# Attention and a routed expert layer on one core: seven zero stores left out and a new written-out order for the attention phase

## The chip, the cores and the metric

The kernel runs on one NeuronCore of a Trainium2 chip. TensorE (PE; its weight loads are PEld in the profile) multiplies, VectorE (DVE), ScalarE (ACT) and GpSimd (POOL) do the rest, and SyncE (SP) issues most transfers; every engine takes its instructions in the order in which they were written. The metric is device time in microseconds (us) of one execution. Where a profile speaks of the granted clock, 1.00 is TensorE at 2.4 GHz.

## The reference

Attention with four sink keys and a window of 128, then a top-2 mixture of eight experts over its 3072 output rows:

```python
scores = scale * np.matmul(q, k.transpose(0, 1, 3, 2))     # 4 x 8 heads, 768 x 768, D = 64
keep = is_sink | in_window                                 # 4 sinks, window of 128
a = softmax(np.where(keep, scores, -1e9))
x = np.matmul(a, v)  -> (3072, 512)
noisy = x @ w_gate + log1p(exp(x @ w_noise)) * noise       # top 2 of 8 per token
for e in range(8): out[mask] += top2_w * (relu(x[mask] @ w1[e]) @ w2[e])   # 512 -> 1024 -> 512
```

All of it is in float32. On TensorE the experts' products are made of three products of split operands (`w` and its rest, `x` and its rest).

## The kernel before

The kernel has two phases. **Phase one** is attention: 16 pairs of heads (`g`), and for each pair three tiles of 256 query rows, so 48 tiles `n`. A tile goes through `qk` (scores, L404), a copy of the scores to `cbuf` (`prev`, L408 on DVE or L410 on ACT, and `cur`, L426), a maximum (`mins`, L433, DVE), its negative (`minus_max`, L436, POOL), the exponential with its sum (`exps_sums`, L447, ACT), a turn on TensorE (`ptr`, L494), a copy back to `CT` (L408/L410), a masked copy `CM` (L507 on DVE or L510 on POOL), the product with `v` (`pv`, L520 and L523; the latter needs `dv`, the differences of neighbouring blocks of `v`, L310 on POOL), the sinks (L535) and a copy to `xtn` (L408/L410). Rows are then turned (`rows`, L549) and stored to a scratch tensor `x_rows` in DRAM (L554).

Four pairs make one batch of 768 tokens. When a batch is done its logits are made (`proj`, `turn`, L735, L743), and `routing` finds each token's two experts and its rank in each expert's list (DVE, POOL and ACT, some 40 small instructions; `rank` L849/L855 and `place` L944 on TensorE; the one-hot tables `rt_op`, L927, on DVE). Its last transfer, `keep` (L873 to L876), stores the gate weights of the batch in four stores of 128 x 6 runs of 48 bytes each. Rows of the first expert are gathered from `x_rows` by POOL (L1029) while attention still runs. The first weight chunks are loaded too (`st`, L1136) and split (`hi`, L1140, ACT; `lo`, L310, POOL).

**Phase two** is the experts: 16 pieces of up to 512 rows, eight up products (L1184 to L1186) and the down products (L1250 to L1252) in each, with gathers of the next piece's rows and a scatter with addition (L1274) of each result into `out`. `out` has 31 tiles of 128 rows, 24 of tokens and 7 behind the last token, into which the unused slots of a list are scattered; the kernel returns the first 3072 rows alone. Tiles of `out` are set to zero beforehand by stores of a zero tile (`zero`, L1427 to L1429), one per tile of 128 rows: the first `ZEROS` in phase one and the others in phase two.

The order of phase one is written out by hand in three tables. `ORDER` lists the numbers of its operations (transfers included) in the order in which `Plan.replay` emits them; `SIDE` has a 1 where an operation with two possible engines takes the second; `BANKS` gives each PSUM buffer its bank. So each engine's queue, SP's too, is a subsequence of `ORDER`. The durations in the calls of `plan.op` and `plan.dma` move nothing in phase one; the order of phase two is computed from such durations, starting from the times at which `replay` leaves the engines.

Of the kernel before, what the change touches and what calls it, by code (L numbers as in the profile page):

```python
# [27 lines left out]
SLACK = .01  # L28
WARM = 32
FIRST = 4  # L30
ZEROS = 16
EARLY = ((1, 0), (1, 1), (2, 0))
LATE = ((2, 1), (1, 2), (1, 3))

# [1 line left out]
def dram(t, off, ap):  # L36
    return bass.AP(tensor=t.tensor, offset=t.offset + off, ap=ap)


ORDER = """  # L40
# [43 lines left out]
"""  # L84
SIDE = """
11011111100111100110100101101110101110000110111010011001111010010000011000010100011001010000010101111001010001010100
1111000100000100000100000100
"""
BANKS = """
00120120120112001210012001201100211020112001120102021002101012110021102001200110002112102010101211020101210201100210  # L90
0112100112110002012101120201012010120110210110102012
"""


# [667 lines left out]
def routing(nc, plan, cst, sh, b, t0, nt, z, xbuf):  # L762
# [5 lines left out]
    last = T0 + nt == sh.T  # L768
    c, get = cst, plan.get
    gid = b  # L770
# [13 lines left out]
    def t(name):  # L784
        if name in ("oh", "z", "r2"):
            return (name, gid)
        if last and name in ys:
            return ("y", ys[name])
        if name == "lg":
            return ("lg", b)  # L790
        tag = "rt_" + name
        plan.rings.setdefault(tag, 1)
        return (tag, gid)
# [81 lines left out]
            nc.sync.dma_start(dram(xbuf, (T0 + 1) * 128 * sh.XW + q * sh.SW + 128, [[sh.XW, 128], [128 * sh.XW, nt], [1, E + C]]),  # L875
                              rt("w")[:, :, q // 2, :])  # L876

    plan.dma(z if last else plan.now, keep, 1.2, r=[t("w")], w=[("wrow", gid)], n=4)
    most = c["most"]
    ends = last or b in sh.fixed  # L880
    if ends:
        i = b
# [314 lines left out]
def experts(tc, plan, cst, sh, w1, w2, xbuf, out):  # L1197


    nc = tc.nc  # L1200
# [6 lines left out]
    plan.rings.update(gw=2, w1=4, w2a=2, w2b=2, skn=2, sqn=2, wc=2, h=FC + 1, y=4, H=2, Y=4)  # L1207
    scat = {}
    NP = sh.B * sh.H // 2
    zeros = range(ZEROS, out.shape[0] // 128)  # L1210
    UP1, DN1 = DC * 3 * (1 / 2400), .69

    def size(e, t):
# [78 lines left out]
    z = 0  # L1292
# [5 lines left out]
    for q, (e, tiles, width) in enumerate(info):  # L1298
# [34 lines left out]
        for f in range(FC):  # L1333
            k = FC * q + f
            zu = z0 + f * dz if not apart else z0 + f * UP1 * width
            if k >= AHEAD:
                for i in range(DC) if q == 0 else (None,):
                    op("PE", (UP1 * width + .19) / (1 if i is None else DC), zu, lambda q=q, f=f, i=i: up(q, f, i),
                       r=[(x, e, t) for x in ("xh", "xl") for t in tiles] + [w_tile(plan, 1, e, f // 2)[0]], w=[("H", k)],
# [7 lines left out]
        for a, t in enumerate(order):  # L1347
            n = Y[e, t]
            for f in range(FC):
# [3 lines left out]
                   r=[("hh", k), ("hl", k), w_tile(plan, 2, e, f // 2)[0]], w=[("Y", n)], u=[("h", k)])  # L1353
# [72 lines left out]
def zero(plan, nc, cst, sh, out, i, z, r):  # L1426

    plan.dma(z, lambda: nc.sync.dma_start(dram(out, i * 128 * sh.DM, [[sh.DM, 128], [1, sh.DM]]), cst["zt"][:, :sh.DM]),
             .73, r=r, w=[("zero", i)])  # L1429


def phase_one(tc, nc, plan, ac, tail, cst, sh, kq, v, vs, w1, w2, xbuf, out):
# [34 lines left out]
        logits(nc, plan, cst, sh, sh.B - 1, jj, n + PR.get("ll", .5))  # L1467
    first_rows(sh.FA - 1, PR.get("ga_l", 0), PR.get("gt_l", 0))
    for i in range(ZEROS):
        zero(plan, nc, cst, sh, out, i, 60, [("xt", 8 + i * 38 // ZEROS)])  # L1470
    plan.dma(12, lambda: nc.sync.dma_start(dram(xbuf, 0, [[sh.XW, 128], [1, sh.XW]]), cst["zt"]), .8,
             r=[("xt", 3)], w=[("blank", 0)])
    for x, (m, i) in enumerate(EARLY):
# [3 lines left out]
    for f in range(AHEAD):  # L1477
        for i in range(sh.DM // 128):
            plan.op("PE", 3 * (128 * FIRST / 2400 + .016), PR.get("ua", 60) + f, lambda f=f, i=i: up_ahead(plan, nc, sh, f, i),
                    r=[(x, 0, t) for x in ("xh", "xl") for t in range(FIRST)] + [w_tile(plan, 1, 0, f // 2)[0]],  # L1480
                    w=[("H", f)], u=[("S", NJ * HP * sh.B)])
# [112 lines left out]
```

## Time and profile before

| What | Value |
|---|---|
| Median of 3 runs | 751.35 us (750.37 to 752.58) |
| The profiled execution, its own time | 750.74 us |
| Span of the profile (first to last instruction) | 749.1 us |
| Granted TensorE clock, mean | 0.991 |
| Busy: PE / DVE / ACT / POOL | 724.6 / 427.3 / 328.8 / 389.5 us |
| Moved by DMA | 97.39 MB |

Between span and the execution's own time lie 1.64 us. Busy time is a share of the whole span; phase one fills about the first 176 us of it and phase two the rest, and the two differ in which engine has spare time.

### The profile page before, as it was taken

The page shows a single profiled execution, that of the slowest core. Times are in us where ns is not written, and L with a number is a line of the kernel's source. Part 1 is how long each engine was busy: PE and PEld are TensorE (multiplying, and loading weights), DVE is VectorE, ACT ScalarE, POOL GpSimd, SP SyncE. Part 2 cuts the span into 40 slices and gives each one's busy share as a digit, 9 for nine tenths or more (in the row PEclk, how much of TensorE's full clock was granted, in tenths as well). Part 3 has the DMA queues.
Part 4 walks back from the last instruction along what each step waited for, and adds up shares of the span by engine and source line. Part 5 has one row for each costly group of instructions (what it writes and reads, how often), then busy time and mean ns, then how long its engine had stood idle before and what let it go on. Part 6 is the DMA issues. An engine that isn't in the chain of part 4 may idle for free.

```text
span 749.1 us, 16784 instructions
## 1 busy us (share of the span) xinstructions
PE 724.6 (97%) x6531; PEld 621.2 (83%) x6531; DVE 427.3 (57%) x1109; ACT 328.8 (44%) x863; POOL 389.5 (52%) x603
## 2 busy tenths in 40 slices
PE   8999897889999999999999999999999999999995
PEld 4877675577889998889888988898898989899994
DVE  7988777767755653654465446535543664463320
ACT  5999893894224423341333143323423341433221
POOL 4545366471257466365727472748283654747212
PEclk9999999799999999999999999999999999999999
DMA  7577686546649644543445364516451763464033
GB/s 272 165 221 228 170 235 201 166 111 156 176 127 202 207 83 77 153 128 56 85 145 133 52 125 134 117 39 158 127 105 25 159 171 57 85 174 74 14 43 44
DMA packets 58643, 97.39 MB, mean 130 GB/s; under 512 B 19280, under 2 KB 32592, under 8 KB 58560
## 3 DMA queue, kind: packets, MB, share of 16 engines
q1 hardware_dynamic: 45248, 68.82, 30.5%
q0 software_dynamic: 13312, 27.46, 20.6%
q8 instruction: 52, 0.85, 0.5%
q14 instruction: 31, 0.25, 0.1%
HBM read 67.92 MB, written 28.34 MB: 129 GB/s over the span
## 4 chain that ended last, share of the span: by engine, by line
PE 80%; ACT 7%; DVE 4%; issue 4%; DMA 2%; POOL 1%; SPq 1%; POOLq 0%; DVEq 0%; ACTq 0%
PE H L1186 12%; PE H L1184 12%; PE H L1185 12%; PE Y L1251 11%; PE Y L1252 11%; PE Y L1250 11%; ACT cbuf L447 3%; PE D L404 2%; PE D L494 2%; PE X L520 2%; ACT CT L410 1%; PE Y L1255 1%; PE Y L1256 1%; PE X L523 1%; POOL out L1274 1%
## 5 line engine op out<-in xcount | busy, mean ns | idle before, releaser
L1035 POOL DMA_INDIRECT xg<-x_rows,rt_idq x173 | 174.5, 1008 | 60.2 <-issue 49.2
L1231 ACT ACTIVATE h<-H 128x384 fp32r<-128x384 f32 (+4 forms) x127 | 63.8, 502 | 263.5 <-PE H L1186 239.0
L1186 PE MATMUL H<-skn,w 128*128 128x384 f32 (+4 forms) x508 | 173.8, 342 | 0.0
L1184 PE MATMUL H<-skn,w 128*128 128x384 f32 (+4 forms) x508 | 173.8, 342 | 0.0
L1185 PE MATMUL H<-sqn,w 128*128 128x384 f32 (+4 forms) x508 | 173.4, 341 | 0.0
L1239 DVE SCALAR_TENSOR_TENSOR h<-H,h 128x384 fp32r<-128x384 f32 (+4 forms) x167 | 74.9, 469 | 169.0 <-ACT h L1231 159.4
L1274 POOL DMA_INDIRECT out<-y,idx x53 | 94.1, 1775 | 53.3 <-ACT y L1259 36.9
L1184 PEld LDWEIGHTS H<-skn,w 128*128 128x128 f32 x508 | 95.4, 188 | 6.5
L1185 PEld LDWEIGHTS H<-sqn,w 128*128 128x128 f32 x508 | 95.3, 188 | 6.3
L1283 POOL COPY spacer<-h 1x1 f32<-1x1 f32 x88 | 25.7, 292 | 140.6 <-ACT h L1231 139.9
L1186 PEld LDWEIGHTS H<-skn,w 128*128 128x128 f32 x508 | 95.3, 188 | 1.7
L447 ACT ACTIVATE cbuf<-cbuf,nb 128x132 f32<-128x132 f32 x192 | 75.3, 400 | 8.0 <-POOL nb L436 4.3
L1252 PE MATMUL Y<-w2a,h 128*128 128x512 f32 x192 | 75.6, 394 | 0.0
L1252 PE MATMUL Y<-w2b,h 128*128 128x512 f32 x192 | 75.6, 394 | 0.0
L1251 PE MATMUL Y<-w2a,h 128*128 128x512 f32 x192 | 75.5, 393 | 0.0
L1251 PE MATMUL Y<-w2b,h 128*128 128x512 f32 x192 | 75.5, 393 | 0.0
L1250 PE MATMUL Y<-w2b,h 128*128 128x512 f32 x192 | 75.0, 391 | 0.0
L1250 PE MATMUL Y<-w2a,h 128*128 128x512 f32 x192 | 74.8, 390 | 0.0
L1102 ACT ACTIVATE skn<-xtn 128x512 fp32r<-128x512 f32 (+2 forms) x46 | 27.8, 604 | 51.1 <-DVE xtn L1093 47.2
L404 PE MATMUL D<-kq 64*64 64x196 f32 (+3 forms) x832 | 41.3, 316 | 2.3 <-DVE CT L408 0.8
L1252 PEld LDWEIGHTS Y<-w2b,h 128*128 128x128 f32 x192 | 36.0, 188 | 7.8
L1252 PEld LDWEIGHTS Y<-w2a,h 128*128 128x128 f32 x192 | 36.0, 188 | 7.7
(214 smaller groups left out, 1198.8 us busy)
## 6 DMA issues: line engine op xcount, KB each, us to landing
st<-in_w1l SPq DMA_DIRECT2D x32, 512.0 KB
st<-in_w2l SPq DMA_DIRECT2D x32, 512.0 KB
kq<-in_kq SPq DMA_DIRECT2D x15, 792.0 KB
out<-zt SPq DMA_DIRECT2D x31, 256.0 KB
vn<-in_v SPq DMA_DIRECT2D x16, 384.0 KB
x_rows<-xr SPq DMA_DIRECT2D x48, 128.0 KB
xg<-x_rows,rt_idq POOLq DMA_INDIRECT x173
out<-y,idx POOLq DMA_INDIRECT x53
```

The source lines that it names most:

```text
L404: nc.tensor.matmul(x[:, o:o + w], kq(g)[r, 1, j, t], k[:, f:f + w], start=True, stop=True)
L447: nc.scalar.activation(C(n)[:, u], C(n)[:, u], AF.Exp, bias=get("nb", n)[:, u:u + 1], scale=1.0 / math.sqrt(D), accum_out=get("sm", n // 2 ...
L1035: nc.gpsimd.indirect_dma_start(out=x[:, i, :], out_offset=None, in_=xbuf.rearrange("r (q d) -> (r q) d", d=sh.SW), in_offset=bass.Indirect ...
L1184: nc.tensor.matmul(p, w[:, 0], xh, start=(i == 0), stop=False)
L1185: nc.tensor.matmul(p, w[:, 0], xl, start=False, stop=False)
L1186: nc.tensor.matmul(p, w[:, 1], xh, start=False, stop=(i == sh.DM // 128 - 1))
L1231: nc.scalar.activation(get("h", FC * q + f, [128, 2 * 128 * FIRST], F32R)[:, :width], H(q, f), AF.Relu)
L1239: nc.vector.scalar_tensor_tensor(h[:, o:o + s1 - s0], p[:, s0:s1], 0.0, h[:, s0:s1].bitcast(F32), op0=OP.max, op1=OP.subtract)
L1250: nc.tensor.matmul(p, hh, w[:, 0], start=(f == 0), stop=False)
L1251: nc.tensor.matmul(p, hh, w[:, 1], start=False, stop=False)
L1252: nc.tensor.matmul(p, hl, w[:, 0], start=False, stop=(f == FC - 1))
L1274: d = nc.gpsimd.indirect_dma_start(out=out, out_offset=bass.IndirectOffsetOnAxis(ap=c["idx"][:size(e, t), e, t:t + 1], axis=0), in_=get("y ...
```

## The change

The diff sets `ZEROS` to 9 and lets the phase-two stores end at `sh.T` (24), so the seven tiles behind the last token are no longer set to zero: 24 stores instead of 31, nine of them in phase one (16 before) and 15 in phase two (15 before). It gives the routing's stores other durations in the plan, and it replaces the three tables. `ORDER` has 14 numbers fewer (a store is an issue and a transfer) and all operations of phase one stand in another sequence.

```diff
-ZEROS = 16
+ZEROS = 9
 ORDER = """
-0 1 8 74 72 9 10 12 2 75 14 11 16 4 18 13 73 20 6 22 15 24 118 26 17 28 30 120 19 32 3 34 173 21 36 38 221 23 40 42
...
+0 1 8 10 4 5 12 14 16 18 20 22 9 13 24 26 28 30 15 32 2 3 6 7 34 36 17 25 38 27 23 40 118 119 19 42 44 46 21 48 89
...
 SIDE = """
-11011111100111100110100101101110101110000110111010011001111010010000011000010100011001010000010101111001010001010100
...
+11011100101010100110101010110001100010101000001100100010110010100010000010011000000000010101100100110100010000110000
...
 BANKS = """
...
-    plan.dma(z if last else plan.now, keep, 1.2, r=[t("w")], w=[("wrow", gid)], n=4)
+    plan.dma(z if last else plan.now, keep, 1.2 if last else 2.2, r=[t("w")], w=[("wrow", gid)], n=4 if last else 6.5)
...
-    zeros = range(ZEROS, out.shape[0] // 128)
+    zeros = range(ZEROS, sh.T)
...
-             .73, r=r, w=[("zero", i)])
+             .9, r=r, w=[("zero", i)])
...
-        zero(plan, nc, cst, sh, out, i, 60, [("xt", 8 + i * 38 // ZEROS)])
+        zero(plan, nc, cst, sh, out, i, 60, [("xt", 8 + round(i * 15 / (ZEROS - 1)) * 38 // 16)])
```

How the tables move instructions is shown at three places. In the rows, line numbers of the changed kernel are one lower (its `ORDER` is one line shorter); `kq` and `vn` are the loads of one pair's keys and queries and of its values, `rt_w` is the source of the routing's four stores, `zt` of a zero store, `xr` of a store of rows, `st` the target of a weight chunk.

First SP's queue about the stores of batch 0. Before, the rows from the loads of pair 11's keys on:

```order
L378 DMA kq_1615<-in_kq 128x1584
L1428 DMA out_0<-zt_100 128x512
L875 DMA x_rows<-rt_w_898 128x6x12 x4
L381 DMA vn_1740<-in_v 128x768
L378 DMA kq_1871<-in_kq 128x1584
L381 DMA vn_1879<-in_v 128x768
```

And now, from the loads of pair 8's values on:

```order
L380 DMA vn_1765<-in_v 128x768
L377 DMA kq_1772<-in_kq 128x1584
L369 DMA vr_1852<-in_vs 16x1024 x2
L380 DMA vn_2019<-in_v 128x768
L377 DMA kq_2123<-in_kq 128x1584
L874 DMA x_rows<-rt_w_1629 128x6x12 x4
L377 DMA kq_2174<-in_kq 128x1584
```

The values of pairs 8 and 9 and the keys of pair 12, which stood behind the four stores, stand ahead of them; behind them comes pair 13's load of keys, and no zero store is near.

Second, SP's queue about the stores of batch 1. Before:

```order
L1428 DMA out_0<-zt_100 128x512
L875 DMA x_rows<-rt_w_1967 128x6x12 x4
L381 DMA vn_2397<-in_v 128x768
L1428 DMA out_0<-zt_100 128x512 x2
L1136 DMA st_2541<-in_w1l 128x1024
L378 DMA kq_2547<-in_kq 128x1584
L381 DMA vn_2582<-in_v 128x768
L381 DMA vn_2705<-in_v 128x768
```

And now:

```order
L380 DMA vn_2455<-in_v 128x768
L377 DMA kq_2513<-in_kq 128x1584
L553 DMA x_rows<-xr_1841 32x8x128 x4
L1135 DMA st_2635<-in_w1l 128x1024
L380 DMA vn_2662<-in_v 128x768
L874 DMA x_rows<-rt_w_2157 128x6x12 x4
L377 DMA kq_2756<-in_kq 128x1584
L380 DMA vn_2795<-in_v 128x768
```

The values of pairs 11 and 12 (`vn_2397`, `vn_2582` before, `vn_2455`, `vn_2662` now) and the second weight chunk (`st_2541` before, `st_2635` now) stood behind the stores and two zero stores, and now stand ahead of them.

Third, ACT's queue about the cast of that second weight chunk (`w1<-st`). Before:

```order
L410 ACTIVATE CT_2549<-D_157 128x512
L527 ACTIVATE ps_2556<-D_157 128x128
L1140 ACTIVATE w1_2620<-st_2541 128x1024
L410 ACTIVATE xtn_2636<-X_155 128x256
L410 ACTIVATE cbuf_95<-D_158 128x4x132
L410 ACTIVATE CT_2673<-D_157 128x512
L527 ACTIVATE ps_2677<-D_157 128x128
```

And now:

```order
L409 ACTIVATE CT_2646<-D_157 128x512
L738 ACTIVATE lt_2659<-D_156 128x256
L526 ACTIVATE ps_2665<-D_157 128x128
L1139 ACTIVATE w1_2679<-st_2635 128x1024
L409 ACTIVATE cbuf_95<-D_158 128x4x132
```

The cast stood behind the sinks' copy `ps` of tiles 32 and 33; now it stands behind that of tiles 34 and 35 and the logits' copy `lt` of batch 2, some two tiles later.

## Rows read from the trace of the kernel before

**Rows 1.** Windows: busy us (count) of each engine, granted clock, DMA share, GB/s.

```profile
10.00:80.00 70.00, 68.94 (x1778) 53.16 (x1776) 64.33 (x177) 63.94 (x276) 35.30 (x92) 1.00 0.70 214
80.00:90.00 10.00, 7.93 (x154) 4.93 (x146) 6.63 (x17) 6.95 (x28) 3.87 (x9) 1.00 0.70 186
90.00:110.00 20.00, 19.26 (x517) 15.14 (x513) 15.39 (x66) 19.80 (x85) 12.31 (x35) 1.00 0.91 247
110.00:150.00 40.00, 31.40 (x643) 22.25 (x640) 30.31 (x82) 25.88 (x97) 23.23 (x41) 0.87 0.62 176
150.00:180.00 30.00, 27.73 (x579) 21.70 (x580) 20.51 (x68) 23.44 (x88) 16.62 (x34) 1.00 0.50 125
180.00:700.00 520.00, 520.00 (x2610) 463.56 (x2609) 279.00 (x670) 177.45 (x278) 284.36 (x366) 1.00 0.49 117
```

**Rows 2.** The same view in steps of ten, 130 to 150 us.

```profile
130.00:140.00 10.00, 6.75 (x102) 4.32 (x105) 6.47 (x20) 6.73 (x32) 5.06 (x10) 0.56 0.93 263
140.00:150.00 10.00, 9.19 (x214) 6.87 (x208) 8.45 (x31) 9.31 (x38) 4.42 (x12) 0.93 0.26 80
```

**Rows 3.** Timeline of SP's queue, 73 to 117 us: start, us, what is issued.

```profile
73.92 5.25 SPq L875 DMA_DIRECT2D x_rows<-rt_w  x4
79.71 0.70 SPq L381 DMA_DIRECT2D vn<-in_v  x1
...
105.41 6.14 SPq L875 DMA_DIRECT2D x_rows<-rt_w  x4
...
115.30 0.50 SPq L1136 DMA_DIRECT2D st<-in_w1l  x1
```

**Rows 4.** Timeline, 84 to 88 us: start, us, instruction, in brackets the idle before.

```profile
84.32 1.54 POOL L310 TENSOR_TENSOR dv<-vn 128x640 f32<-128x640 f32 x1 [3.44 <-PE D L404]
...
87.10 0.41 ACT L447 ACTIVATE cbuf<-cbuf,nb 128x132 f32<-128x132 f32 x1 [2.19 <-POOL nb L436]
```

**Rows 5.** Timeline, 122 to 134 us.

```profile
122.17 1.06 ACT L1140 ACTIVATE w<-st 128x1024 fp32r<-128x1024 f32 x1 [5.95 <-DMA st<-in_w1l]
...
128.07 3.12 DVE L927 TENSOR_TENSOR rt_op<-io,rt_pp 128x768 f16<-128x768 f32 x2
...
131.60 0.72 PE L944 MATMUL D<-rt_tc,rt_op 128*128 128x56 f16 x12 [3.27 <-DVE cbuf L426]
...
133.00 1.23 POOL L1029 DMA_INDIRECT xg<-x_rows,idg  x1 [2.62 <-DMA x_rows<-xr]
```

**Rows 6.** Timelines of SP's queue and of PE, the first 16 us.

```profile
0.93 0.87 SPq L370 DMA_DIRECT2D vr<-in_vs  x2
...
2.31 2.61 SPq L378 DMA_DIRECT2D kq<-in_kq  x4
...
6.42 0.81 PE L404 MATMUL D<-kq 64*64 64x132 f32 x20 [0.45 <-DMA kq<-in_kq]
...
14.95 1.16 PE L494 MATMUL D<-idf,cbuf 64*64 64x64 f32 x64
...
21.22 0.61 PE L364 MATMUL X<-one 128*128 128x512 bf16 x2
```

**Rows 7.** Timeline about the end of phase one, 175 to 182 us.

```profile
175.32 0.41 SPq L1136 DMA_DIRECT2D st<-in_w1l  x1
...
180.88 1.05 ACT L1140 ACTIVATE w<-st 128x1024 fp32r<-128x1024 f32 x1
```

**Rows 8.** The zero stores' line: count, ns min/median/max, first and last start.

```profile
L1428 SPq DMA_DIRECT2D out<-zt x31: 349/432/1617, 41.8 to 244.0; - x31
```

**Rows 9.** Groups of ACT by form, 0 to 178 us: busy us, mean ns | idle before.

```profile
L410 ACT ACTIVATE CT<-D 128x512 f32<-128x512 f32 x39 | 23.0, 588 | 2.4 <-PE D L494 2.2
L410 ACT ACTIVATE cbuf<-D 128x528 f32<-128x528 f32 x22 | 13.3, 607 | 7.6 <-PE D L404 7.5
L410 ACT ACTIVATE xtn<-X 128x256 f32<-128x256 f32 x27 | 9.4, 375 | 3.3 <-PE X L535 3.2
L482 ACT ACTIVATE pcbuf<-cbuf 64x32 f32<-64x32 f32 x36 | 8.3, 232 | 0.3
```

More of the change, by code (lines that the diff above doesn't have):

```diff
@@ L40 @@
 ORDER = """
[43 rows of a table removed]
[42 rows of a table added]
 """
 SIDE = """
-11011111100111100110100101101110101110000110111010011001111010010000011000010100011001010000010101111001010001010100
-1111000100000100000100000100
+11011100101010100110101010110001100010101000001100100010110010100010000010011000000000010101100100110100010000110000
+0101000101000111001101101100
 """
 BANKS = """
-00120120120112001210012001201100211020112001120102021002101012110021102001200110002112102010101211020101210201100210
-0112100112110002012101120201012010120110210110102012
+01021020120110201201010201210011021002112001212001201201010120110021102100200110010122102100101210101201100212010120
+1012100110120120201102102101200110121100210110102012
 """
```

83 rows, old and new, of the table ORDER are left out of this document.

## The prediction

> **What bounds it now.** I first read the windows, to see where TensorE runs out of work. From 180 to 700 us PE is busy 520.00 of 520.00 us at full clock [rows 1]. Whatever is saved before 180 us therefore moves all of that forward unchanged, and nothing that other engines do behind 180 us counts, unless it makes PE wait. So the question is what phase one loses. From 10 to 80 us PE is idle 70.00 - 68.94 = 1.06 us and from 90 to 110 us 0.74 us: 1.80 us in 90, a calm rate of 0.020 us lost per us. From 80 to 90 it loses 2.07 us, from 110 to 150 it loses 8.60, from 150 to 180 it loses 2.27 [rows 1]. The clock is a second loss in the third of these. In 130 to 140 us only 0.56 of full clock is granted, in the next ten 0.93 [rows 2]; 6.75 us of PE work there would have taken 0.56 of that at full clock and 9.19 would have taken 0.93, so 2.97 + 0.64 = 3.61 us more are lost. Together 2.07 + 8.60 + 3.61 + 2.27 = 16.55 us in the 80 us from 80 to 90 and from 110 to 180.
>
> Then I read what each loss waits for, on the engines around PE. POOL sits idle 3.44 us before the `dv` of pair 8 at 84.32 [rows 4]. The row names PE as releaser, but the values that this `dv` subtracts were issued only at 79.71, directly behind four stores of the routing that held SP's queue for 5.25 us from 73.92 [rows 3]. POOL's small operations stand behind that `dv`, so ACT's exponentials then wait 2.19 us for `nb` [rows 4], and PE has nothing to turn. It is one chain: stores, load, `dv`, exponentials, PE.
>
> At batch 1 the same happens with more behind it. The four stores hold the queue 6.14 us from 105.41; the second weight chunk is issued at 115.30 [rows 3], and ACT, in whose queue its cast stands, waits 5.95 us for it, until 122.17 [rows 5]. All tiles are late then, two `rt_op` take DVE 3.12 us in one piece, PE waits 3.27 us for that row of work, and POOL waits 2.62 us for stored rows at its first gather [rows 5]. After PE has been this idle the granted clock falls [rows 2].
>
> **The change, part by part.** *The queue's order at batches 0 and 1.* Nothing that is needed soon stands behind the routing's stores any more: the values of pairs 8 and 9, and of 11 and 12, and the second weight chunk are issued ahead of them. The cast of that chunk has also moved some two tiles down ACT's queue. If a load takes as long as that one did, 122.17 - 115.30 = 6.87 us, two tiles (some 3.6 us each, 176 us over 48 tiles) about cover it, besides the earlier issue. So I take both named waits, 3.44 us on POOL and 5.95 us on ACT, as gone.
>
> What comes in their place can't be read from an order. Its bounds are the two rates above. At the calm rate the 80 us lose 80 x 0.020 = 1.6 us, and 16.55 - 1.6 = 14.95 us are saved. At the rate of 150 to 180 us, where routing is done too but no load is late (2.27 / 30 = 0.076), they lose 6.05 us, and 10.5 us are saved. I take the latter: these stretches hold routing, gathers and weight splits, as that one does, and the calm ones mostly don't. The other end, nothing saved, is a rival.
>
> *The start.* The first keys were issued behind `vr` and `vn`, at 2.31 us, and are now first in the queue, at about 0.93: up to 1.4 us earlier for the first scores at 6.42 [rows 6]. Against that, 23 instead of 19 of the 32 filler products (`X<-one`) now stand behind the first scores, 15 of them right ahead of the first `ptr`, which ran at 14.95 [rows 6]. Four more at 0.61 / 2 = 0.3 us [rows 6] are 1.2 us where PE isn't waiting anyway. I cost the start at 0, with bounds of 1.4 us gained and 1.2 lost.
>
> *The seven zero stores.* Seven issues at the median of 0.43 us [rows 8] are 3.0 us of SP's queue, and 7 x 0.26 = 1.8 MB of traffic. I give them no time of their own. The scatters come late in phase two, where PE is never short; in phase one they are among what stood about the routing's stores, so their worth is inside the waits above. If that cover weren't there, 3.0 us of queue would be the most.
>
> *Moves between engines.* By the tables ACT gains six copies to `CT` and four to `xtn`, and gives six copies to `cbuf` to DVE and five pairs of `pcbuf` copies to POOL: 6 x 0.588 + 4 x 0.375 - 6 x 0.607 - 10 x 0.232 = -0.93 us [rows 9]. I cost it at nothing, since ACT has spare time outside 90 to 110 us; there it is busy 19.80 of 20 us [rows 1], so at most 0.9 us is gained.
>
> *The end of phase one.* The load of chunk (2,1) stood ahead of two zero stores and four stores of rows, and now stands directly ahead of the last chunk's, which was issued at 175.32 and cast at 180.88 without idle time before it [rows 7]. The last chunk then lands later by one transfer: 0.52 MB at the 214 to 247 GB/s of [rows 1] is 2.1 to 2.5 us. ACT waits that long, and the last batch's routing stands behind these casts. The up and down products have other chunks to work on, so I put 0.5 us of it on the path, between 0 and 2.5.
>
> Sum against the profiled execution's own time: 750.74 - 10.5 - 0 + 0.5 = 740.7 us. The median of the runs is 0.6 us above that execution, so the forecast is 741.3 us. At the calm rate and with the other terms at their best it would be 750.74 - 14.95 - 1.4 - 0.9 + 0.6 = 734.1.
>
> A rule that speaks against the main term: the four stores carry 36 KB each and hold the queue 5.25 and 6.14 us [rows 3]. The Trainium skill, page "DMA: Bandwidth & Descriptors", section "Issuing engines are not separate DMA queues", says that the time on the sequencer to initiate a transfer is usually small relative to the transfer itself. By that rule the place of these stores in the queue would not matter, and the time would be that of the first rival. The two rows contradict it for stores of this shape.
>
> **Rivals.** *The transfers, not the queue (same).* If late loads are late because the DMA engines are full, issuing them earlier only lets them wait there. For it: DMA share 0.91 from 90 to 110 us [rows 1] and 0.93 in 130 to 140 [rows 2]. Against it: 0.62 over 110 to 150 us, in which the worst loss lies [rows 1], and the loads that stood right behind the stores. It leaves about 1 us of gain: 750.3.
>
> *Half of it.* One of the two batches still stalls, because another in-order wait turns up there: 110 to 150 us keeps half of its 12.21 us. That gives 741.3 + 6.1 - 1.5 (half of what I let these 40 us lose anyway) = 745.9, and from there up to 749.
>
> *All of it.* The calm rate holds throughout: 734 to 738.
>
> *Slower: the first gathers.* POOL's three gathers wait for the four stores of batch 1. In POOL's queue the first gather stood 31 rows behind the last write of `rt_w`; now it is 16. The stores (6.14 us [rows 3]) now also stand behind the load of pair 12's values, which waits for PE. While POOL waits, the `nb` of the next tiles stand behind it, ACT and PE run dry, and the clock falls as in [rows 2]. Then the 9.2 us that I save in 110 to 150 are lost (12.21 less 40 x 0.076), which leaves 0.8 saved, and every us of that wait beyond the 2.62 of [rows 5] is added. With a wait of 8 us: 750.74 - 0.8 + 5.4 + 0.6 = 755.9. From 5.7 us on the kernel is slower than before by more than 0.3%. Against it: the 16 rows hold a `dv` (1.54 us [rows 4]) and several tensor operations of weights and tables, so the stores have most of their time covered.
>
> **How the numbers follow.** 0.3%, about 2.25 us, is what a measurement of this kernel can tell from no change: 749.1 to 753.6. Chances: the forecast with its own range 738 to 745, 0.50; half of it, 745 to 749, 0.13; all of it, below 738, 0.15; same, 0.12; slower, 0.10. Faster is 0.50 + 0.13 + 0.15 = 0.78. The range reaches from 735.5, so as to take in most of the case at the calm rate, to 750.0, which leaves out the slower case and most of the same one, some 0.2 in all.
>
> **What would show it.** Right: no wait of ACT for `st<-in_w1l` above 1 us, no POOL idle of 3 us before a `dv` behind the first routing's stores, PE idle in the 40 us that answer to 110 to 150 at most 4 us, granted clock 0.99 or more in each ten us of phase one, the first expert product (176 us before) near 166, and 520 us of 520 in phase two as before. The start is right if the first `ptr` stands within 1 us of 14.95. Wrong: a POOL wait of over 5 us before the first gather with the clock at 0.5 to 0.6 behind it, or the routing's stores taking their 5 to 6 us while the loads issued ahead of them still land late. PE idle behind 180 us would make the end term wrong.

## The result and the profile after

The changed kernel takes 743.35 us (median of 18 runs, 739.37 to 750.52) where the kernel before takes 750.10 us in the same sessions (18 runs, 747.17 to 756.69). The ratio is 0.9901 with a 95% interval of 0.9876 to 0.9925: faster by 1.0%, some 7 us. One of the 18 runs of the changed kernel (750.52 us) counts as a slow one and is left out of the ratio. The two profiled executions differ a little more: the span falls from 749.1 to 739.7 us, by 9.4.

The windows of the changed kernel, cut as [rows 1] and [rows 2] (busy us and count of each engine, granted clock, DMA share, GB/s):

```profile
10.00:80.00 70.00, 68.03 (x1800) 55.38 (x1803) 59.85 (x164) 64.50 (x272) 38.47 (x96) 1.00 0.63 199
80.00:90.00 10.00, 9.90 (x250) 6.84 (x242) 9.58 (x25) 9.64 (x43) 5.80 (x15) 1.00 0.65 147
90.00:110.00 20.00, 18.84 (x532) 16.20 (x528) 16.68 (x70) 18.84 (x76) 13.40 (x37) 1.00 0.80 227
110.00:150.00 40.00, 35.33 (x821) 27.03 (x811) 34.90 (x103) 34.91 (x140) 27.54 (x57) 0.96 0.77 175
150.00:180.00 30.00, 27.48 (x346) 21.15 (x347) 23.69 (x83) 15.01 (x41) 10.66 (x19) 1.00 0.61 164
180.00:700.00 520.00, 519.63 (x2587) 463.41 (x2586) 271.65 (x630) 174.93 (x274) 283.69 (x365) 1.00 0.48 115
...
120.00:130.00 10.00, 7.65 (x182) 5.25 (x184) 7.67 (x23) 7.17 (x31) 6.89 (x11) 0.92 0.87 273
130.00:140.00 10.00, 9.29 (x196) 7.20 (x192) 9.28 (x35) 8.70 (x35) 6.33 (x14) 0.91 0.49 114
```

From 80 to 90 us PE loses 0.10 us where it lost 2.07, and from 110 to 150 it loses 4.67 where it lost 8.60; the clock's dip is shorter: it stood at its lower level (0.50, that is 1.2 GHz) for some 10 us and does now for some 3.4, as the windows below show. The calm stretches got a little worse: 1.97 against 1.06 us from 10 to 80, 1.16 against 0.74 from 90 to 110. Phase two is as full as before.

SP's queue about the routing's stores of batches 0 and 1, which answers to [rows 3]:

```profile
81.83 0.35 SPq L380 DMA_DIRECT2D vn<-in_v  x1
82.22 0.43 SPq L377 DMA_DIRECT2D kq<-in_kq  x1
82.75 4.29 SPq L874 DMA_DIRECT2D x_rows<-rt_w  x4
...
106.94 1.28 SPq L1135 DMA_DIRECT2D st<-in_w1l  x1
112.62 0.36 SPq L380 DMA_DIRECT2D vn<-in_v  x1
113.08 2.61 SPq L874 DMA_DIRECT2D x_rows<-rt_w  x4
```

The loads stand ahead of the stores, as the order said. ACT and PE wait for these things in phase one (view of the waits, 10 to 180 us: total us, times, longest):

```profile
ACT w2a L1139 <- DMA st<-in_w2l: 1.2, 1, 1.2
...
ACT w L1139 <- DMA st<-in_w1l: 0.2, 1, 0.2
...
PE D L493 <- issue: 1.8, 5, 0.5
PE D L493 <- ACT ps L526: 1.3, 1, 1.3
PE D L403 <- issue: 1.3, 2, 1.0
PE D L403 <- DVE cbuf L425: 1.2, 3, 0.7
PE X L534 <- issue: 0.9, 1, 0.9
PE X L848 <- DVE m L839: 0.7, 1, 0.7
```

ACT's wait of 5.95 us for the second weight chunk [rows 5] is gone: that chunk is cast at 117.39 us without a wait, and the 0.2 us belong to a later chunk, cast at 171.75. Nothing in POOL's list is a `dv` that waits for a load. A part of what PE still loses is new: "issue", time in which it waited for nothing that the profile shows. PE's own timeline gives three marks, and the last line has the first expert product of the kernel before:

```profile
15.33 0.39 PE L493 MATMUL D<-idf,cbuf 64*64 64x64 f32 x10
...
70.19 0.39 PE L403 MATMUL D<-kq 64*64 64x196 f32 x4 [1.03 <-issue]
...
165.19 0.50 PE L1183 MATMUL D<-skn,w 128*128 128x512 f32 x1
...
176.33 0.50 PE L1184 MATMUL D<-skn,w 128*128 128x512 f32 x1
```

The first `ptr` comes at 15.33 us (14.95 before), the first expert product at 165.19 (176.33 before), 11.1 us earlier, of which 9.4 are left at the end. By busy time these 9.4 us are 24.5 - 20.0 = 4.5 us less idle time of PE (span less busy time, 749.1 - 724.6 and 739.7 - 719.7) and 4.9 less busy time for the same 6531 products. Windows that end at the first expert product, with 3700 products ahead of it in both kernels, and over the stretch at the lower clock, tell more (first the kernel before, then the changed one):

```profile
0.00:176.33 176.33, 159.57 (x3700) 117.61 (x3700) 140.88 (x427) 141.30 (x568) 95.49 (x226) 0.97 0.66 192
131.15:141.30 10.15, 8.05 (x128) 5.34 (x127) 5.82 (x20) 8.02 (x38) 5.47 (x11) 0.50 0.85 250
...
0.00:165.19 165.19, 153.67 (x3700) 119.22 (x3700) 139.34 (x417) 141.28 (x562) 98.35 (x236) 0.99 0.67 189
128.45:131.80 3.35, 3.08 (x56) 2.36 (x58) 3.03 (x6) 2.94 (x14) 2.94 (x7) 0.50 0.22 81
```

PE's idle time ahead of that product falls from 16.8 to 11.5 us, by 5.2. At half the clock half of the busy time is lost: 8.05 / 2 = 4.0 us before and 3.08 / 2 = 1.5 now, 2.5 less. What is left, 159.57 - 4.03 = 155.5 us and 153.67 - 1.54 = 152.1, is the busy time of the same 3700 products at full clock: 3.4 us less. These three make the 11.1 us. Worked out the same way, this busy time lies between 153.6 and 155.8 us in all eight profiles of the old sequence (the kernel before and its seven edited versions below) and between 150.4 and 152.1 in all six of the new one. So this part goes with the sequence of the engines, and no edit of a wait below takes it out of its range; what in the sequence does it is not shown. Behind the first expert product 1.7 us are given back.

Beside their times, the runs list their mean granted clock. Over the 98 runs made beside the experiments the kernel before has 0.9908 on average (0.983 to 0.996), over 17 runs the changed kernel has 0.9952 (0.991 to 0.998). An estimate from these: (0.9952 - 0.9908) x 740 us = 3.3 us, so at most about half of the 7 us is clock. It is an upper estimate, for the mean also counts the lower clock while PE is idle; in the profiled pair the clock has 2.5 of the 9.4 us.

### The profile page after: what moved, and what is told of

The parts are those of the page before. It is cut to its first block, busy times and chain, and to the rows that moved or that the text cites. A ratio compares the mean times of both kernels' runs of the same rounds, so it can differ in the third digit from the quotient of the medians.

```text
span 739.7 us, 16786 instructions
## 1 busy us (share of the span) xinstructions
PE 719.7 (97%) x6531; PEld 622.6 (84%) x6531; DVE 426.7 (58%) x1105; ACT 328.6 (44%) x857; POOL 392.0 (53%) x613
## 4 chain that ended last, share of the span: by engine, by line
PE 80%; ACT 5%; issue 5%; DMA 4%; DVE 2%; POOL 2%; SPq 1%; POOLq 0%; ACTq 0%; DVEq 0%
PE H L1185 11%; PE H L1184 11%; PE H L1183 11%; PE Y L1250 11%; PE Y L1251 11%; PE Y L1249 10%; PE D L403 3%; PE D L493 3%; PE X L519 2%; ACT cbuf L446 2%; DMA st<-in_w1l 2%; PE X L522 2%; PE X L534 2%; POOL out L1273 2%; PE Y L1254 1%
## 5 line engine op out<-in xcount | busy, mean ns | idle before, releaser
L1171 DVE TENSOR_TENSOR gw<-xg,perm 32x8 f32<-32x8 f32 x173 | 27.2, 157 | 30.6 <-DMA xg<-x_rows,rt_idq 23.7
```

## Experiments

The theory at the start was that of the prediction: loads that are soon needed stood behind the routing's stores in SP's queue, and the new place of these loads brings the gain. Its rivals: the zero stores' traffic, and the sequence of the other engines. The ratio is to the kernel before; the clock is the mean over the kernel's runs.

| Kernel | us, median | Ratio, 95% interval | Clock |
|---|---|---|---|
| changed kernel | 743.35 | 0.9901 [0.9876, 0.9925] | 0.9952 |
| e1 before, seven zero stores out | 748.96 | 0.9991 [0.9969, 1.0012] | 0.9902 |
| e2 changed, all 31 zero stores | 744.09 | 0.9920 [0.9892, 0.9948] | 0.9939 |
| e3 before, loads ahead | 757.86 | 1.0106 [1.0080, 1.0133] | 0.9837 |
| e4 changed, loads behind | 744.92 | 0.9932 [0.9910, 0.9954] | 0.9928 |
| e5 before, `ri` ahead | 750.15 | 1.0004 [0.9984, 1.0024] | 0.9922 |
| e6 before, `ri` ahead and `place` later | 752.94 | 1.0040 [1.0016, 1.0063] | 0.9894 |
| e7 before, stores a little later | 749.89 | 1.0007 [0.9986, 1.0027] | 0.9898 |
| e8 changed, `ri` behind | 746.37 | 0.9963 [0.9938, 0.9987] | 0.9933 |
| e9 before, e1 + e5 + e7 | 746.41 | 0.9939 [0.9911, 0.9968] | 0.9912 |
| e10 changed, e4 + e8 | 743.94 | 0.9903 [0.9873, 0.9932] | 0.9954 |
| e11 changed, zero stores all late | 744.97 | 0.9920 [0.9890, 0.9950] | 0.9937 |
| e12 before, e5 + e7 | 747.57 | 0.9983 [0.9964, 1.0002] | 0.9919 |

### The zero stores by themselves

e1 takes seven of the 16 stores of phase one out of the old sequence, e2 gives the changed kernel its seven back, in phase two.

```diff
+TILE = {7: 5, 11: 6, 14: 7, 15: 8}
-        zero(plan, nc, cst, sh, out, i, 60, [("xt", 8 + i * 38 // ZEROS)])
+        zero(plan, nc, cst, sh, out, TILE.get(i, i), 60, [("xt", 8 + i * 38 // ZEROS)])
-    zeros = range(ZEROS, out.shape[0] // 128)
+    zeros = range(9, sh.T)
```

```diff
-    zeros = range(ZEROS, sh.T)
+    zeros = range(ZEROS, out.shape[0] // 128)
```

> The kernel before with its own sequence, but without the seven zero stores that stand about the routing's stores (its 6th, 7th, 9th, 10th, 11th, 13th and 14th; the nine that stay zero tiles 0 to 8, phase two 9 to 23). Queue theory (loads lost time because they stood behind the routing's four stores): the four stores still take 4 us or more at batches 0 and 1, POOL still waits 2.5 us or more before pair 8's dv and ACT 4 us or more for the second weight chunk; 747 to 750 us. Rival, traffic: the zero stores fill the DMA engines and so slow the routing's stores and the loads; without them the four stores take under 2.5 us, both waits fall under 1 us and the time to 741 to 745 us.

> The changed kernel with all 31 tiles set to zero: 22 zero stores in phase two in place of 15, phase one untouched. Queue theory: as the changed kernel, ratio to it within 0.3%, 742 to 745 us, and phase two without PE idle from 190 to 690 us. Rival, the stores themselves cost: seven more issues of 0.43 us and 1.8 MB show as 1.5 to 3 us, 745 to 747 us.

Neither moves the time beyond its interval, as the queue theory said. But e1 was a first warning: the four stores still held SP's queue for 4.58 and 5.42 us, and yet ACT's wait for the second chunk had shrunk from 5.95 to 1.3 us and POOL's before pair 8's `dv` from 3.44 to 2.58, without a gain in time. ACT's wait was below the 4 us that the queue theory had named. Each profile is one execution, and this wait differs between profiles of the same queue: in e5 and e6 below, which leave SP's queue as it was, it is 2.69 and 0.41 us, and neither is faster than the kernel before.

### The queue's order by itself

e3 moves the routing's stores behind the loads in the old kernel, e4 moves them ahead of the loads in the new one. In both nothing else moves.

```diff
 SP's queue of e3, batch 1
-L875 DMA x_rows<-rt_w 128x6x12 x4
 L381 DMA vn<-in_v 128x768
 L1428 DMA out<-zt 128x512 x2
 L1136 DMA st<-in_w1l 128x1024
 L378 DMA kq<-in_kq 128x1584
+L875 DMA x_rows<-rt_w 128x6x12 x4
```

```diff
 SP's queue of e4, batch 1
+L874 DMA x_rows<-rt_w 128x6x12 x4
 L553 DMA x_rows<-xr 32x8x128 x4
 L1135 DMA st<-in_w1l 128x1024
 L380 DMA vn<-in_v 128x768
-L874 DMA x_rows<-rt_w 128x6x12 x4
 L377 DMA kq<-in_kq 128x1584
```

> The kernel before with nothing moved but two places in SP's queue: the routing's stores of batch 0 now stand behind the loads of pair 12's keys and pair 9's values, those of batch 1 behind the load of the second weight chunk. All 31 zero stores stay, and every other engine keeps its sequence. Queue theory: POOL's wait of 3.44 us and ACT's of 5.95 us fall under 1.5 us each, granted clock 0.97 or more in each ten us, and most of the gain is there: 741 to 745 us. Rival, the sequence of the other engines is what helped: the two waits may go, but PE loses the time elsewhere between 80 and 180 us and the time stays at 747 to 750 us.

> The changed kernel with nothing moved but the routing's stores in SP's queue: those of batch 0 directly behind the last write of their source in the written-out order, ahead of the loads of pair 9's values and pair 12's keys; those of batch 1 likewise, ahead of the second weight chunk and pair 12's values. Queue theory: the second weight chunk is issued 5 us or more later, ACT waits 2 us or more for it, the clock falls under 0.9 for some us, and the time goes back to 747 to 751 us. Rival, the sequence of the other engines: the time stays within 0.3% of the changed kernel, 742 to 745 us.

e3 is slower by 1.06%, which no theory had foreseen. The cause is in POOL's timeline of e3:

```profile
99.81 0.22 POOL L867 COPY rt_w<-ri 128x48 f32<-128x48 f32 x1 [11.42 <-DMA x_rows<-rt_w]
```

The stores of batch 0 now also stood behind four stores of rows, and their source `rt_w` is written again for batch 1 by this copy. POOL waited 11.42 us for them, and PE was busy for 2.14 of the 10 us from 90 to 100, with the clock at 0.77. So e3 can't decide on the theory, but it shows the price of a store that is issued too late.

e4 is a fair test, and the theory fails in it. Its queue and ACT's waits:

```profile
104.88 7.63 SPq L874 DMA_DIRECT2D x_rows<-rt_w  x4
112.61 2.02 SPq L553 DMA_DIRECT2D x_rows<-xr  x4
114.67 0.47 SPq L1135 DMA_DIRECT2D st<-in_w1l  x1
...
ACT w L1139 <- DMA st<-in_w1l: 3.8, 2, 3.6
```

The stores hold the queue for 7.63 us, the chunk is issued at 114.67 instead of 106.94, ACT waits 3.6 us for it, POOL waits 3.04 us for the values of pair 9 before their `dv`, and the mean clock from 120 to 130 us is 0.74. So the stalls of before are back, and yet the time rises by some 2 us of the 7 (the intervals of the two kernels overlap) and not by all of them.

e7 repeats e3 without that flaw: the stores of batch 0 stand behind pair 8's values alone, those of batch 1 directly behind the weight chunk.

```diff
 SP's queue of e7, batch 0
-L875 DMA x_rows<-rt_w 128x6x12 x4
 L381 DMA vn<-in_v 128x768
+L875 DMA x_rows<-rt_w 128x6x12 x4
 L378 DMA kq<-in_kq 128x1584
```

> The queue test without the wait that spoiled the first one: the kernel before with the stores of batch 0 behind pair 8's values alone and those of batch 1 directly behind the second weight chunk, so that both are done long before their source is written again. Queue theory: POOL's wait before pair 8's dv and ACT's for the second chunk fall under 1.5 us, and the time to 742 to 746 us. Theory of the small instruction: both waits fall just as much, but PE gets back only what they cost by themselves, 0.9 us from 80 to 90 and some 1 us from 110 to 130; place still waits 3 us, the clock still falls, 748 to 750 us.

SP's queue of e7, and further down its windows and PE's waits:

```profile
76.18 0.33 SPq L381 DMA_DIRECT2D vn<-in_v  x1
76.63 3.52 SPq L875 DMA_DIRECT2D x_rows<-rt_w  x4
...
107.27 0.47 SPq L1136 DMA_DIRECT2D st<-in_w1l  x1
109.22 5.17 SPq L875 DMA_DIRECT2D x_rows<-rt_w  x4
...
120.00:130.00 10.00, 8.02 (x114) 5.01 (x109) 5.66 (x14) 2.84 (x7) 4.55 (x6) 0.74 0.50 149
130.00:140.00 10.00, 7.37 (x133) 4.66 (x130) 7.69 (x20) 7.55 (x38) 5.87 (x11) 0.58 0.83 218
...
PE X L520 <- issue: 3.4, 2, 2.0
PE D L944 <- DVE cbuf L426: 1.8, 1, 1.8
```

The chunk is issued 8 us earlier than in [rows 3], ACT doesn't wait for it at all, and pair 8's `dv` doesn't wait either. PE is busy for 8.84 us from 80 to 90 (7.93 before). The time is that of the kernel before (1.0007). From 120 to 140 us PE has other gaps, and the mean clock falls to 0.74 and 0.58. Two of PE's gaps are "issue" (1.41 us, ended at 111.34, and 1.98 us, ended at 123.19), which the profile of before doesn't have, and POOL waits 3.22 us, until 128.65, for the values of a later pair, for which it waited 0.55 before; pair 12's load still stands behind the stores here. So the two waits that the prediction took as the cause are gone, and the loss has stayed, but in part as other waits; what the queue's order is worth without these e7 doesn't show.

### A small instruction on DVE

In the old sequence ACT's exponentials of tile 36 wait 3.29 us for the reciprocal `ri` of pair 15 (0.19 us), which stands on DVE behind the two `rt_op` of [rows 5]:

```profile
131.72 0.41 ACT L447 ACTIVATE cbuf<-cbuf,nb 128x132 f32<-128x132 f32 x1 [3.29 <-DVE ri L474]
```

e5 moves it ahead of them; e6 also moves PE's `place`, which waits for the `rt_op`, behind the next `ptr`; e8 moves `ri` and the second `rt_op` the other way in the changed kernel.

```diff
 DVE's queue of e5
+L474 RECIPROCAL ri<-sm 128x4x2
 L917 TENSOR_SCALAR rt_pp<-rt_g 128x12
 L549 STREAM_TRANSPOSE xr<-xtn 128x8x32
 L927 TENSOR_TENSOR rt_op<-io,rt_pp 128x768
 L927 TENSOR_TENSOR rt_op<-io,rt_pp 128x768
 L426 COPY_PREDICATED cbuf<-le,D 128x4x64
-L474 RECIPROCAL ri<-sm 128x4x2
```

> The kernel before with one instruction moved: on DVE, the reciprocal ri of pair 15 (0.19 us) stands ahead of the two rt_op of batch 1 (with the small operation and the turn ahead of them) instead of behind them. Theory of the small instruction: ACT's exponentials of tile 36 wait 3.29 us for this ri (they reuse the sm buffer that it reads), so that wait falls under 0.5 us, PE has the turn of tile 36 ready when its place is over, and 2 to 4 us come back with the better clock: 746 to 748.5 us. Queue theory: the late loads make all tiles late, the place of ri doesn't matter, 749 to 751 us.

> As the run with ri ahead, and PE's place of batch 1 also stands behind the next tile's ptr instead of ahead of proj and ptr (its three index operations on DVE, the first gather on POOL and one proj move with it). Theory of the small instruction: PE then turns tile 36 while DVE makes the one-hot tables, the wait of 3.27 us before place falls under 1 us, granted clock 0.97 or more from 130 to 150, and 4 to 6 us come back: 744 to 746.5 us. Queue theory: 749 to 751 us.

> The changed kernel with two DVE instructions of batch 1 moved towards where they stood before: the second rt_op directly behind the first, and ri of pair 15 behind both. SP's queue is untouched. Theory of the small instruction: ACT's exponentials of tile 36 wait 1 to 3 us for ri, PE runs dry for 1 to 2 us about 115 to 122, and the time rises to 744.5 to 748 us. Queue theory: nothing but noise, 742 to 745 us.

e5 gains nothing (1.0004), although ACT no longer waits for `ri` and the wait before `place` is 1.7 us instead of 3.27. e6 is slower by 0.4%: `place` waits no more, but the `ptr` ahead of it now waits 3.4 us itself. e8 does rise, to 0.9963, but not for the reason given: ACT shows no wait for `ri` in its profile. The longest gap of PE there is of another kind, some 15 us ahead of the moved instructions:

```profile
97.86 0.38 PE L534 MATMUL X<-ps,vr 16*128 16x128 f32 x2 [2.29 <-issue]
```

The profiled execution of e8 took 742.45 us, 3.9 less than the median of its runs, so what the slower ones lost is not in this profile. As the cause by itself this theory falls with e5.

### Several at once

The theory left is that at batch 1 several in-order waits end within a few us of each other, so that taking one away only lets the next one show. e9 puts e1, e5 and e7 together, e12 leaves e1 out of that, and e10 puts e4 and e8 together in the changed kernel.

> The kernel before with three edits at once that gained nothing one by one: without the seven zero stores about the routing's stores, with the routing's stores behind pair 8's values and the second weight chunk, and with ri of pair 15 ahead of the two rt_op. Theory of parallel waits: at batch 1 several in-order waits end within a few us of each other, so taking one away leaves the next; with all three gone PE idle from 110 to 150 falls from 8.60 to under 5 us, the clock stays at 0.95 or more in each ten us, and the time is 743 to 746.5 us. Rival, the sequence as a whole: the old order leaves PE short there whatever single wait is taken out, 748 to 750.5 us.

> The three edits to the kernel before without the first of them: the routing's stores moved behind the loads and ri moved ahead of the two rt_op, but all 31 zero stores kept, seven of them about the routing's stores. If the zero stores are one of the parallel waits, the gain of the three edits goes: 748.5 to 750.5 us. If their traffic is nothing beside the two waits, the time stays at that of the three edits: 745 to 747.5 us.

> The changed kernel with both undoings at once: the routing's stores ahead of the loads again, and the second rt_op and ri of pair 15 moved back on DVE. Theory of parallel waits: ACT waits 3 us or more for the second weight chunk and the two losses do not add up, since one wait hides the other: 745.5 to 748 us. Rival, two independent losses: they add to 747.5 to 750 us.

The three edits that gained nothing one by one gain 0.6% together (0.9939), over half of the change's gain; none of the three intervals by itself reaches that far (the lowest end is 0.9969). Windows of e9:

```profile
110.00:120.00 10.00, 8.95 (x257) 7.30 (x255) 9.08 (x22) 6.65 (x17) 8.85 (x16) 1.00 0.61 138
120.00:130.00 10.00, 7.34 (x120) 4.46 (x116) 7.73 (x22) 6.33 (x27) 6.95 (x7) 0.89 0.72 194
130.00:140.00 10.00, 9.54 (x176) 7.22 (x178) 7.44 (x22) 8.14 (x34) 5.46 (x15) 0.77 0.57 172
140.00:150.00 10.00, 9.13 (x269) 7.31 (x264) 8.63 (x43) 9.94 (x44) 6.32 (x20) 1.00 0.34 57
```

PE's idle time from 110 to 150 falls from 8.60 to 5.04 us, just short of the 5 expected, and the clock still dips to 0.77, where 0.95 was expected. e9 and e10 ran in one session, in which the kernel before took 751.28 us at a mean clock of 0.9894. e9 has 0.9912, e10 0.9954, and e10 is 746.41 - 743.94 = 2.5 us faster; by the upper estimate from above the clock alone would make (0.9954 - 0.9912) x 740 = 3.1 us of that. So clock may be all that e9 lacks, but that is not shown: in the profiles e9 also needs 153.6 us of busy time at full clock for the 3700 products, as the other versions of the old sequence do, and e10 150.4.

Without the zero stores' edit most of it goes: e12 has 0.9983. The intervals of e9 and e12 touch at 0.9964 to 0.9968, so that the seven stores are worth some 3 us here is likely rather than certain. By themselves, in e1, they were worth nothing.

e10 has 0.9903, the time of the changed kernel, though the stores are ahead of the loads again, hold the queue for 6.81 us from 104.03, and ACT waits 2.1 us for the chunk. POOL waits 2.18 us again for pair 9's values. The new sequence carries these waits. Neither of the two times expected for e10 (745.5 to 748, 747.5 to 750) came, so the theory of parallel waits, which e9 bears out, did not foresee this one. That e8, a part of e10, is slower than e10 by 0.6% has no explanation in the edits and stays open.

### The zero stores that are left

> The changed kernel with none of its zero stores in phase one and all 24 in phase two. Theory that full DMA engines hold up PE's instructions (the gaps of 0.3 to 1 us in the middle of a row of products, for which the profile names nothing): with 2.36 MB less in phase one the gaps near 70 and 126 us shrink, PE idle from 110 to 150 falls from 4.67 to under 4 us, and the time to 740.5 to 743 us. Rival: the gaps stay, since loads and rows of x fill the engines anyway, and the time stays at 743 to 745 us.

```diff
-    zeros = range(ZEROS, sh.T)
+    zeros = range(sh.T)
```

In e11 the last zero stores, at 251.5 us, come behind the first scatters, at 226.8, so some rows miss their first addend; the work of the engines is the same. The time is 744.97 us (0.9920), no better than the changed kernel, and its profile has more "issue" gaps than before the edit, not fewer (2.45 us at 77 us, 2.01 at 103). That profile is of its slowest run (751.08 us), so the number of gaps in it may be above the usual; the median speaks for the rival.

## Why the prediction came out

The number was right: 741.3 us forecast, 743.35 measured, well inside 735.5 to 750.0 and inside the likeliest case's own range of 738 to 745. The reason given for it was right only in part.

- **What bounds it.** Right. PE is busy 519.63 of 520 us from 180 to 700, and the gain was made ahead of that.
- **The main term, 10.5 us.** The first expert product is 11.1 us earlier. That the size came so near is luck: two errors cancel in it. The 80 us lose 0.10 + 4.67 + 1.45 + 2.52 = 8.7 us and not 6.05 (1.45 is the clock's part, 7.65 x 0.08 + 9.29 x 0.09), and the calm stretches 1.3 more, so 16.55 - 8.7 - 1.3 = 6.5 us were saved there and not 10.5. Against that stand the 3.4 us of busy time, which the sum didn't have.
- **The queue's order as the cause.** This is the step that failed: "Nothing that is needed soon stands behind the routing's stores any more", and so both waits go and the loss with them. The waits did go, but e7 takes the same two out of the old sequence and gains nothing, and e4 and e10 put the queue back in the new one, with waits of 2 to 4 us on ACT and POOL, and lose some 0.3% (e4, with overlapping intervals) or nothing (e10). The chain stores, load, cast, PE was in the trace, but beside it stood others that ended at nearly the same time: DVE's two `rt_op` ahead of `ri` and PE's `place`. Of the versions of the old sequence only the one with three edits (e9) gained anything. The change gave all engines another sequence, and with it came the 3.4 us of busy time that no edit of a wait brought.
- **The start, 0.** Right: the first `ptr` is 0.4 us later, within the 1 us allowed.
- **The zero stores, 0 with 3.0 us at most.** Right alone (e1, e2). In company their worth was likely at the upper end given, some 3 us (e9 against e12, whose intervals touch).
- **Moves between engines, 0.** Not tested by itself; nothing in the profile speaks against it.
- **The end of phase one, 0.5 us.** Mis-sized: of the 11.1 us 1.7 are given back behind the first expert product, inside the 0 to 2.5 given. The waits in that place are ACT's 1.2 us for `st<-in_w2l` and PE's 0.7 for the routing's `m`.
- **What would show it.** The clock was to be 0.99 or more in each ten us and PE's idle time 4 us at most in 110 to 150; they are 0.91 and 4.67. The waits of ACT and POOL, the first product near 166 us and the full phase two came as said.
- **The rivals.** The transfers-not-the-queue case would have left the time unchanged. "Slower" named the first gathers on POOL; they wait 0.71 us. But its mechanism, POOL behind late stores of `rt_w`, is what e3 ran into at another instruction, for 11.42 us.
- **The rule weighed.** The Trainium skill, page "DMA: Bandwidth & Descriptors", section "Issuing engines are not separate DMA queues", has the time to initiate a transfer as usually small. The same four stores held the queue for 2.61 us in the changed kernel and 7.63 in e4, so four together can hold up what stands behind them. A single one took the queue 0.37 to 2.06 us in e4 (median 0.55) and landed 2.7 to 7.7 us after its issue (median 6.6), which agrees with "usually small" relative to the transfer: the prediction's "contradict it" was too strong. What the rule would have made of the place of these stores, nothing, is near what e7 and e10 measured, though not for its reason, since the waits in e4 did come back.

What is not settled is the clock's part. The changed kernel and e10 have 0.995, the other versions of the new sequence 0.993 to 0.994, all versions of the old one 0.984 to 0.992. Which of the moves keeps PE from the gap that lets the clock fall was not found, nor which of them shortens the busy time.

## What to carry to other kernels

A wait that the profile names is worth its length only if nothing else ends just behind it: before building on it, take it out alone, and then together with its neighbours, for three edits of no worth each were worth 0.6% together here. One profile is one execution: the wait of 5.95 us, on which the prediction built, was 0.41 to 2.69 us in three other profiles with these stores in the same place. A store that is moved back in a queue holds its source: look for the next write of that tile first.

## What was unexpected of the hardware

PE stops in the middle of a row of products with nothing to wait for that the profile shows, and in most cases starts again about 2.4 us after one packet of the profile's instruction queue. PE's timeline of e12 at such a place:

```profile
120.95 0.65 PE L520 MATMUL X<-CT,vn 128*64 128x128 f32 x7
124.13 0.27 PE L520 MATMUL X<-CT,vn 128*64 128x128 f32 x1 [2.53 <-issue]
```

Seven of eight products were done, and the eighth came 2.53 us later. The DMA view of e12 from 121.75 to 122.00 us, where the data packets had just ended:

```profile
DMA packets 1, 0.02 MB, mean 66 GB/s; under 512 B 0, under 2 KB 0, under 8 KB 0
## 3 DMA queue, kind: packets, MB, share of 16 engines
q8 instruction: 1, 0.02, 24.1%
```

The profiles of the changed kernel and the twelve experiments have 28 such gaps of 0.7 us or more on PE between 16 and 180 us. The profiles of the kernel before and of e4 have none. In 24 of the 28 the last packet of q8 starts 2.29 to 2.53 us ahead of the gap's end, in three 2.8 to 3.4, in one 5.1; a moment taken at random in this stretch lies 2.2 to 2.55 us behind such a packet in 6% of all cases, so this is hardly chance. Most packets are followed by no such gap: every profile has 52 of them, about 29 between 13.5 and 180 us. In 21 of the 28 the hardware queue took over 75% of the DMA engines in the 2.5 us ahead of the gap, where a moment taken at random has that in about 46%. The profile of the changed kernel counts 52 packets of q8 with 0.85 MB, and 13,062 matmuls and weight loads on PE, 251 for each packet, which is why I take them for PE's instructions; that a packet is late because data stands ahead of it is argued from these rows and was not shown, and e11, with less traffic, had no fewer gaps. The Trainium skill, page "Runtime: NRT & Kernel Launch", section "Instruction fetch mechanics", has each engine's instructions come in blocks of 16 KiB through a DMA queue of its own, at a cost that is mostly hidden. The size agrees with the profile (0.85 MB / 52 = 16 KB); the cost, if these gaps are it, is not always hidden: up to 2.5 us at a time. All "issue" waits of PE in phase one of the changed kernel come to 4.7 us, of which two gaps of this kind (1.03 and 0.92 us) are 1.95. The clock can fall behind such a gap (in e7 it is at 0.50 from 124.8 to 138.4 us, just behind the second one). Whether the gaps make up much of the 11 us between the fastest and the slowest run of one kernel is not shown; the profile of the kernel before has none, and its run of 750.74 us was no fast one.
